# u of batches 2 to 7 as seven half-size products; one buffer for w_out and the weight sums, refilled from a DRAM copy; x's sums in the gates' place

## The chip, the core and the metric

The kernel runs on one core of a Trainium2 chip. The metric is the device time of one execution in microseconds (us), taken as the median of several runs. Five engines work side by side: PE (matrix products, with its weight loads shown as PEld), DVE (VectorE), ACT (ScalarE), POOL (GpSimd) and SP (SyncE, which here only issues transfers). Each runs its own instructions in a fixed order and waits on semaphores for the others.

## What is computed

Attention without a softmax, then a gated feed-forward block, all in float32:

```python
kv = einsum('bhsd,bhse->bhde', k, v)          # 8 batches, 8 heads, 576 x 64
out = einsum('bhsd,bhde->bhse', q, kv)
x = out / sqrt(mean(out**2, -1) + 1e-6) * g_norm   # then laid out as [8, 576, 512]
h = maximum(x @ w_in, 0)                      # w_in 512 x 1024
u, v = h[..., :512], h[..., 512:]
v_n = (v - mean(v)) / sqrt(var(v) + 1e-6)
v_s = einsum('ts,bsd->btd', w_spatial, v_n) + b_spatial[None, :, None]
result = (u * v_s) @ w_out                    # w_out 512 x 512
```

## The kernel before

**Precision by splitting.** For batches 1 to 7 every large matrix is held as a high part and a low part in a reduced format (names end in H and L: `XH`, `XL`, `WIH`, `WIL`, `VH`, `VL`, `GH`, `GL`, `WOH`, `WOL`). A product is then three PE products, high times high, high times low, low times high (`hl`, L286). A split is two instructions (`split`, L319): ACT copies the value to the high part, DVE subtracts that from the value and writes the low part. Batch 0 is computed in plain float32 by lines of its own while the weights arrive.

**Stages of a batch.** 576 tokens are four tiles of 128 and a tail of 64, the tail being treated together with that of the neighbouring batch. `hv` (L307) makes v for one tile, 12 products of 512 columns; `hv_end` (L325) applies the relu on ACT, the layer norm (statistics and scaling on DVE) and the split, and `sums` (L338) forms sums of V's quarters on DVE. `u_unit` (L408) makes a 128 x 288 block of u: for each of the four 128-row pieces of the contraction three products of 288 columns, 12 in all, in one PSUM bank, from which ACT writes the relu into `U`. There are 8 such units in a batch, 96 products. `sp_steps` (L453) is the spatial product, already in the seven-product (Strassen-Winograd) form, 14 steps over two halves `q`, with `tail_product` for the tail; `gate` (L434) multiplies with `U` on DVE and splits the result into `GH` and `GL`. `out_unit` (L511) multiplies with w_out, and ACT and SP carry the result out.

**Attention between.** `first` (L762: hv and u), `second` (L782: spatial) and `last` (L788: out) call `step` (L706) between their units; each `step` runs one piece of the attention of the next batches (`att_k`, `att_qa`, `att_t`). `att_qa` squares on ACT and sums per head on DVE (`norm_a`, L181: one 512-wide square, then a `TENSOR_REDUCE`); batch 0's first units use the other form in it, eight 64-wide squares on ACT that also accumulate, and no reduction.

**Order and buffers.** A scheduler places the instructions of each engine from the program order and the dependencies. PSUM banks for `hv`, `u`, spatial and out come from one pool of four (`ps_mm`), the attention's from another of three. `WIH`/`WIL` hold w_in for the whole run, `WOH`/`WOL` w_out, `GH`/`GL` the gates. All transfers are issued by SP.

## Time and profile before

| | |
|---|---|
| median of 3 runs | 517.86 us (517.69 to 518.56) |
| the profiled execution's own time | 517.55 us |
| its span, first to last instruction | 515.8 us |
| granted PE clock, mean over the span | 0.999 |
| PE busy | 505.7 us, 98% of the span |
| DVE busy | 359.9 us, 70% |
| ACT busy | 236.4 us, 46% |
| POOL busy | 8.5 us |

The span is covered by PE nearly without a gap from 86 us on. The first 86 us are batch 0 and the decoding of the weights, the stretch from 86 to 164 us is batch 1, and from there each batch takes 54 to 64 us according to how much attention lies in it. "Busy" of DVE and ACT counts time in which at least one instruction is in flight; the instructions of one engine overlap a little, so that a sum of single durations is larger than the busy time.

### The profile page before, as it was taken

How to read it: one execution, taken by the hardware profiler on the slowest of the kernel's cores; microseconds unless marked ns; L12 is line 12 of the kernel's file. 1: busy time of each engine (PE TensorE's matmuls, PEld its weight loads, DVE VectorE, ACT ScalarE, POOL GpSimd, SP SyncE). 2: the span in 40 equal slices, each digit the busy share in tenths (PEclk: the TensorE clock that was granted, in tenths of full speed). 3: DMA queues.
4: the chain of work that ended last, by engine and by line, in shares of the span. 5: the costliest groups of instructions: out<-in, count | busy, mean ns of one | idle time of the engine just before them, and what ended most of it. 6: DMA issues, size and time to landing. Idle time of an engine off the chain costs nothing.

```text
span 515.8 us, 9316 instructions
## 1 busy us (share of the span) xinstructions
PE 505.7 (98%) x3508; PEld 447.5 (87%) x3508; DVE 359.9 (70%) x1076; ACT 236.4 (46%) x572; POOL 8.5 (2%) x23
## 2 busy tenths in 40 slices
PE   7999999999999999999999999999999999999996
PEld 6648777898988899889998899989998899988995
DVE  3898599798952889556692698818694488938470
ACT  2555455865533465335443366325442356434321
POOL 5000000000000000000000000000000000000000
PEclk9999999999999999999999999999999999999999
DMA  8995300423253002112416301220223201020003
GB/s 258 328 323 186 104 24 1 154 67 114 103 191 116 1 1 65 68 39 93 144 35 199 110 22 56 83 104 21 80 80 138 69 0 43 2 81 1 1 0 102
DMA packets 22303, 46.48 MB, mean 90 GB/s; under 512 B 2866, under 2 KB 7474, under 8 KB 22260
## 3 DMA queue, kind: packets, MB, share of 16 engines
q1 hardware_dynamic: 22260, 45.91, 27.5%
q8 instruction: 27, 0.44, 0.4%
q14 instruction: 16, 0.13, 0.1%
HBM read 36.46 MB, written 9.44 MB: 89 GB/s over the span
## 4 chain that ended last, share of the span: by engine, by line
PE 91%; DMA 3%; ACT 3%; DVE 2%; issue 1%; SPq 0%; ACTq 0%
PE pso L284 19%; PE psu L284 16%; PE psh L317 14%; PE psb L423 6%; PE pso L204 5%; PE psc L423 4%; PE psa L423 4%; PE pskv L129 4%; PE psu L391 3%; PE pstr L232 2%; PE psa L400 2%; DMA stage<-w_in 2%; PE psh L367 2%; PE psh L284 2%; PE pst L157 1%; DMA KV<-kvm 1%
## 5 line engine op out<-in xcount | busy, mean ns | idle before, releaser
L284 PE MATMUL psu<-XH,WIH 128*128 128x288 f32 x224 | 66.6, 297 | 0.4 <-ACT U L414 0.4
L284 PE MATMUL psu<-XL,WIH 128*128 128x288 f32 x224 | 66.1, 295 | 0.0
L284 PE MATMUL psu<-XH,WIL 128*128 128x288 f32 x224 | 66.0, 295 | 0.0
L284 PE MATMUL pso<-WOH,GH 128*128 128x512 f32 x144 | 57.0, 398 | 0.0
L284 PE MATMUL pso<-WOL,GH 128*128 128x512 f32 x144 | 56.6, 393 | 0.0
L284 PE MATMUL pso<-WOH,GL 128*128 128x512 f32 x144 | 53.8, 396 | 0.0
L450 ACT CAST GH<-g 128x288 fp32r<-128x288 f32 (+2 forms) x84 | 26.6, 350 | 45.7 <-DVE g L442 45.3
L296 DVE BATCH_NORM_STATS2 s<-v 128x6 f32<-128x512 f32 x32 | 22.0, 692 | 35.8 <-ACT v L290 35.7
L317 PE MATMUL psh<-WIL,XH 128*128 128x512 f32 x112 | 43.7, 391 | 0.0
L317 PE MATMUL psh<-WIH,XH 128*128 128x512 f32 x112 | 43.7, 395 | 0.0
L317 PE MATMUL psh<-WIH,XL 128*128 128x512 f32 x112 | 43.3, 391 | 0.0
L284 PEld LDWEIGHTS psu<-XH,WIH 128*128 128x128 f32 x224 | 42.0, 188 | 1.0 <-ACT U L414 0.6
L284 PEld LDWEIGHTS psu<-XL,WIH 128*128 128x128 f32 x224 | 42.1, 188 | 0.3
L284 PEld LDWEIGHTS psu<-XH,WIL 128*128 128x128 f32 x224 | 42.0, 188 | 0.0
L191 DVE TENSOR_REDUCE ss<-x 128x8 f32<-128x512 f32 x38 | 25.9, 683 | 18.4 <-ACT x L190 18.2
L321 DVE TENSOR_TENSOR VL<-v,VH 128x512 fp32r<-128x512 f32 (+1 forms) x56 | 33.9, 620 | 5.1 <-ACT VH L320 4.6
L414 ACT ACTIVATE U<-psu 128x288 f32<-128x288 f32 x56 | 22.8, 412 | 29.1 <-PE psu L284 28.1
L320 ACT CAST VH<-v 128x512 fp32r<-128x512 f32 (+1 forms) x56 | 30.5, 564 | 11.5 <-DVE v L343 5.8
L524 ACT COPY o<-pso 128x512 f32<-128x512 f32 x35 | 19.7, 589 | 35.1 <-PE pso L284 27.8
L284 PEld LDWEIGHTS pso<-WOH,GL 128*128 128x128 f32 x144 | 27.0, 188 | 5.7
L284 PEld LDWEIGHTS pso<-WOL,GH 128*128 128x128 f32 x144 | 27.1, 188 | 5.0
L284 PEld LDWEIGHTS pso<-WOH,GH 128*128 128x128 f32 x144 | 27.0, 188 | 4.7
(188 smaller groups left out, 1204.1 us busy)
## 6 DMA issues: line engine op xcount, KB each, us to landing
KV<-kvm SPq DMA_DIRECT2D x31, 512.0 KB, 4.9
out<-o SPq DMA_DIRECT2D x32, 256.0 KB, 2.2
qt<-qT SPq DMA_DIRECT2D x16, 288.0 KB, 2.9
stage<-w_in SPq DMA_DIRECT2D x8, 512.0 KB, 6.3
qt<-qT SPq DMA_DIRECT2D x16, 256.0 KB, 2.7
KT<-kvt SPq DMA_DIRECT2D x32, 64.0 KB, 4.7
stage<-w_out SPq DMA_DIRECT2D x4, 512.0 KB, 5.7
stage<-wsT SPq DMA_DIRECT2D x4, 288.0 KB, 4.4
```

Of the source, the lines that this page charges most:

```text
L129: return nc.tensor.matmul(ps[h:h + D, at:at + D], of[:, 0, h:h + D], of[:, 1, h:h + D], start=c == 0, stop=c == NC)
L191: nc.vector.tensor_reduce(ss, heads(x), axis=AX.X, op=ALU.add)
L204: nc.tensor.matmul(ps[:, c * P:(c + 1) * P], qt[:, c * P:(c + 1) * P], st[p], start=True, stop=True)
L284: nc.tensor.matmul(ps, lt, rh, start=i == 0, stop=i == n - 1)
L296: nc.vector.bn_stats(s6, v)
L317: nc.tensor.matmul(ps, lt, rh, start=k == 0 and i == 0, stop=k == NP - 1 and i == 2)
L320: nc.scalar.copy(hi, x)
L321: nc.vector.tensor_tensor(lo, x, f32(hi), op=ALU.subtract)
L414: nc.scalar.activation(U[:, d, cols], ps[:, 0:HS], AF.Relu)
L423: nc.tensor.matmul(ps, lt, rh, start=start and i == 0, stop=stop and i == len(pairs) - 1, skip_group_check=True)
L450: nc.scalar.copy(GH[:, d, dst], g[:, src])
L524: nc.scalar.copy(o, ps)
```

## The change

u of batches 2 to 7 is made by the seven-product scheme that the spatial product has: x (as two by two blocks, halves of the contraction by halves of the tokens) times w_in's u half (as two by two blocks). A step takes 6 products of 288 columns (two 128-row pieces by three), and 14 steps make a batch: 84 products where there were 96.

- Weights. `WIH`/`WIL` are divided into `WVH`/`WVL` (v half) and `WUH`/`WUL` (u half, four blocks). `w_sums` forms the four weight sums once, in batch 1 (two calls): on DVE from high and low part, split again; one sum takes the place of a block no longer needed, three go to DRAM (`spare_u`, 1.57 MB) by SP.
- One buffer `WO` for two uses. w_out's parts are also written to DRAM (`spare_o`, 2.10 MB). In each batch from 2 on, `to_u` takes the buffer under the name `UX` and loads `spare_u` as two transfers of 0.79 MB; `to_out` takes it back and loads `spare_o` as two transfers of 1.05 MB. These four transfers a batch are issued by POOL.
- x's sums. `x_sums` forms per batch, on DVE, 8 additions of high and low part and 8 additions or subtractions, and splits four sums of two pieces each (8 ACT copies, 8 DVE subtractions). They lie in `T`, which has the place of the gates' buffer `G`, and in the rest of `UX`. `T` may be written when the last `out_unit` of the batch before has read `G`, and `G` again when u has read `T`. The tails of the gates move to a small buffer `GT`.
- u's steps. Per batch 4 ACT copies (two of `p1`, two of a finished block) and 10 DVE sums out of PSUM take the place of 8 relus on ACT. A bank is used by up to three steps: its next products wait until the DVE sum that reads the last ones is done. The relu is done in `gate`: `max(U, 0) * v_s` in one instruction.
- Moved from DVE to ACT: the scaling of the layer norm in `hv_end` (with one small DVE product more), the tails' `TB` copies, and for batches 2 to 7 the sums of squares in `att_qa`, now the accumulating form, eight squares and no reduction.

```diff
 def att_q(b, p, st):
-        att_qa(b, p, st)
+        att_qa(b, p, st, b > 1 and True)
...
-        layer_norm(ps, v, nc.vector)
+        layer_norm(ps, v, nc.scalar)
...
+    def x_sums_():
+        for k in range(2):
+            q = []
+            for of, j, name in ((0, 0, "p1"), (2, 1, "u2"), (0, 1, "u3"), (2, 0, "g")):
+                q.append(work.tile([P, HS], F32, name=name, tag=name))
+                x = [f32(x[:, of + k, j * HS:(j + 1) * HS]) for x in (XH, XL)]
+                nc.vector.tensor_tensor(q[-1], *x, op=ALU.add)
+            q11, q22, q12, q21 = q
+            nc.vector.tensor_tensor(q11, q12, q11, op=ALU.subtract)
+            nc.vector.tensor_tensor(q12, q22, q12, op=ALU.subtract)
+            nc.vector.tensor_tensor(q22, q22, q11, op=ALU.subtract)
+            nc.vector.tensor_tensor(q21, q21, q22, op=ALU.subtract)
+            for n, x in (1, q22), (0, q11), (2, q12), (3, q21):
+                split(TH[n][:, k], TL[:, n, k], x)
...
+        def p1(q):
+            ps = bank(q, "a")
+            u_product(ps, q, 0, 0)
+            nc.scalar.copy(temp(q, "p1"), ps)
+        def p2(q):
+            ps = st.pop((q, "a"))
+            u_product(ps, q, 1, 1, False)
+            nc.scalar.copy(own(q, 0, 0), ps)
+        def p6(q):
+            ps = bank(q, "b")
+            u_product(ps, q, 3, 4)
+            nc.vector.tensor_tensor(temp(q, "u2"), ps, st[q, "p1"], op=ALU.add)
+        def p5(q):
+            ps = bank(q, "c")
+            u_product(ps, q, 6, 3)
+        def p7(q):
+            ps = st[q, "b"]
+            u_product(ps, q, 4, 5, False)
+            nc.vector.tensor_tensor(temp(q, "u3"), ps, st[q, "p1"], op=ALU.add)
+            nc.vector.tensor_tensor(own(q, 1, 1), st[q, "c"], st.pop((q, "u3")), op=ALU.add)
+        def p4(q):
+            ps = st.pop((q, "b"))
+            u_product(ps, q, 2, 6, False)
+            nc.vector.tensor_tensor(own(q, 1, 0), ps, st.pop((q, "p1")), op=ALU.add)
+        def p3(q):
+            ps = st.pop((q, "c"))
+            u_product(ps, q, 5, 2, False)
+            nc.vector.tensor_tensor(own(q, 0, 1), ps, st.pop((q, "u2")), op=ALU.add)
...
-        nc.vector.tensor_tensor(g, ps, U[:, d, cols], op=ALU.mult)
+        nc.vector.scalar_tensor_tensor(g, U[:, d, cols], 0.0, ps, op0=ALU.max, op1=ALU.mult)
...
+    def to_u():
+        t = pool_g.tile([P, 7, 2, HS], F32R, name="T", tag="G")
+        x = pool_o.tile([P, 12 * HF + S], F32R, name="UX", tag="WO")
...
+        for i in range(2):
+            nc.gpsimd.dma_start(UX[:, i], spare_u[:, i])
+    def to_out():
+        main_g()
+        main_o()
+        for i in range(2):
+            nc.gpsimd.dma_start(WO[:, i], spare_o[:, i])
...
     def first(b):
+        if b > 1:
+            to_u()
+            x_sums()
         for c in (0, 2, 1, 3):
             hv(b, c)
             step()
...
+        for n, f in enumerate(u_steps()):
...
+        to_out()
```

**How the instructions stand.** On PE, where u of batch 6 ends and the spatial product begins, before:

```order
L284 MATMUL psu<-XH,WIH 128x288
L284 MATMUL psu<-XL,WIH 128x288
L284 MATMUL psu<-XH,WIL 128x288
L423 MATMUL psa<-WSH,VH 128x288
L423 MATMUL psa<-WSL,VH 128x288
```

and on PE in the second half of u of batch 6, with the change (`psua`, `psub`, `psuc` are the banks of the three step families):

```order
L544 MATMUL psua<-XH,WUL 128x288
L544 MATMUL psub<-T,WUL 128x288
L544 MATMUL psuc<-T,UX 128x288 x6
L544 MATMUL psub<-T,WUH 128x288 x2
L544 MATMUL psub<-T,WUL 128x288
L544 MATMUL psub<-T,WUH 128x288 x2
L544 MATMUL psub<-T,WUL 128x288
L544 MATMUL psub<-T,UX 128x288 x6
L544 MATMUL psuc<-T,UX 128x288 x6
L544 MATMUL psub<-T,UX 128x288 x6
L544 MATMUL psub<-UX,WUH 128x288
```

Three products a piece in an unbroken row of 96 have become steps of six on banks that several steps share, and these banks now pass through DVE and ACT between two steps.

On ACT, in u of batch 6, before (from the relu of v's last tiles on; `psu` is u's bank):

```order
L290 ACTIVATE v<-psh 128x512
L166 ACTIVATE sv<-mv,epsc 128x1
L290 ACTIVATE v<-psh 128x512
L414 ACTIVATE U<-psu 128x288
L166 ACTIVATE sv<-mv,epsc 128x1
L320 CAST VH<-v 128x512
L414 ACTIVATE U<-psu 128x288 x2
L362 CAST TA_90<-v 64x512
L362 CAST TA_91<-v 64x512
```

and with the change (`psua` is the bank of the first step families, `x,ss<-pso` one accumulating square):

```order
L499 COPY p_5365<-psua 128x288
L295 ACTIVATE v<-psh 128x512
L504 COPY U<-psua 128x288
L192 ACTIVATE x,ss<-pso 128x64 x6
L171 ACTIVATE sv<-mv,epsc 128x1
L192 ACTIVATE x,ss<-pso 128x64
L171 ACTIVATE sv<-mv,epsc 128x1
L192 ACTIVATE x,ss<-pso 128x64 x8
L171 ACTIVATE sh<-ss,epsc 128x8
L504 COPY U<-psua 128x288
```

Between the two copies out of `psua` now stand fifteen squares of two attention units and three square roots.

On DVE, where the gates of batch 6 end and the layer norm of batch 7 begins, before:

```order
L451 TENSOR_TENSOR GL<-g,GH 128x64
L196 TENSOR_TENSOR x<-pso,rh 128x512
L440 TENSOR_TENSOR g<-psc,u_5200 128x288
L451 TENSOR_TENSOR GL<-g,GH 128x288
L442 TENSOR_TENSOR g<-g,U 128x288
L451 TENSOR_TENSOR GL<-g,GH 128x224
L451 TENSOR_TENSOR GL<-g,GH 128x64
L226 SCALAR_TENSOR_TENSOR XL<-pstr,gcol,XH 128x512
L296 BN_STATS s_5381<-v 128x6
L297 BN_AGGR mv<-s_5381 128x2
```

and with the change (`p`, `u` and `g` without `psc` are x's sums):

```order
L438 TENSOR_TENSOR u_5855<-XH,XL 128x288
L441 TENSOR_TENSOR u_5837<-u_5835,u_5837 128x288
L441 TENSOR_TENSOR u_5857<-u_5855,u_5857 128x288
L326 TENSOR_TENSOR G<-g,G 128x224
L326 TENSOR_TENSOR GT<-g,GT 128x64
L442 TENSOR_TENSOR u_5835<-u_5835,p_5833 128x288
L442 TENSOR_TENSOR u_5855<-u_5855,p_5853 128x288
L438 TENSOR_TENSOR g<-XH,XL 128x288
L443 TENSOR_TENSOR g<-g,u_5835 128x288
L443 TENSOR_TENSOR g<-g,u_5855 128x288
L301 BN_STATS s_5888<-v 128x6
L302 BN_AGGR mv<-s_5888 128x2
```

x's additions have come in between the last gates and the first statistics; the eight subtractions that write `T` stand some 20 rows further down, behind the statistics of v's second tile. On POOL the two transfers into `UX`, the copy of x's tail that was there before (in even batches) and the two into `WO` follow each other.

## Rows read from the trace of the kernel before

**Rows 1.** The page, busy time of each engine (share of the span) and instructions.

```profile
PE 505.7 (98%) x3508; PEld 447.5 (87%) x3508; DVE 359.9 (70%) x1076; ACT 236.4 (46%) x572; POOL 8.5 (2%) x23
```

**Rows 2.** Waits of PE over the whole span: us in total, times, longest.

```profile
PE pskv L129 <- DMA KV<-kvm: 2.1, 2, 1.8
...
PE psu L284 <- ACT U L414: 0.4, 1, 0.4
```

**Rows 3.** Busy us (and instructions) in the stretches of batches 4 to 7.

```profile
283.40:342.64 59.24, 59.24 (x408) 54.47 (x407) 43.61 (x136) 27.86 (x65) 0.40 (x1) 1.00 0.24 78
342.64:404.28 61.64, 61.64 (x484) 56.44 (x483) 39.51 (x121) 25.40 (x61) 0.00 (x0) 1.00 0.25 78
404.28:461.21 56.93, 56.93 (x361) 52.37 (x361) 43.74 (x135) 27.75 (x64) 0.40 (x1) 1.00 0.09 29
461.21:515.80 54.59, 50.64 (x305) 45.92 (x303) 27.72 (x79) 18.29 (x44) 0.00 (x0) 0.99 0.10 34
```

**Rows 4.** The same by stage: out of batch 6, then hv, u, spatial of batch 7.

```profile
449.80:461.20 11.40, 11.40 (x58) 9.61 (x57) 5.58 (x19) 3.83 (x9) 0.00 (x0) 1.00 0.13 47
...
461.21:472.11 10.90, 10.90 (x51) 9.02 (x50) 6.68 (x24) 4.18 (x9) 0.00 (x0) 1.00 0.13 48
472.11:484.82 12.71, 12.71 (x98) 12.71 (x98) 9.43 (x25) 6.54 (x15) 0.00 (x0) 1.00 0.00 0
484.82:500.39 15.57, 15.57 (x112) 15.15 (x111) 9.74 (x26) 4.52 (x13) 0.00 (x0) 1.00 0.00 1
```

**Rows 5.** Pieces of the chain that ended last: start us, us, what.

```profile
439.12 0.89 PE pso L204 x8
...
461.21 10.89 PE psh L317 x48
472.11 12.72 PE psu L284 x96
```

**Rows 6.** Groups by form: count, busy us, mean ns, idle before and its end.

```profile
L191 DVE TENSOR_REDUCE ss<-x 128x8 f32<-128x512 f32 x38 | 25.9, 683 | 18.4 <-ACT x L190 18.2
...
L414 ACT ACTIVATE U<-psu 128x288 f32<-128x288 f32 x56 | 22.8, 412 | 29.1 <-PE psu L284 28.1
...
L442 DVE TENSOR_TENSOR g<-g,U 128x288 f32<-128x288 f32 x42 | 19.0, 453 | 0.5
...
L190 ACT ACTIVATE x<-pso 128x512 f32<-128x512 f32 x31 | 18.4, 599 | 12.1 <-PE pso L204 10.8 <-PE pstr L232 1.1
...
L300 DVE TENSOR_SCALAR v<-v,mv,rv 128x512 f32<-128x512 f32 x32 | 17.3, 543 | 0.7
```

**Rows 7.** DVE in order of time, a stretch without idle time: start, us.

```profile
444.34 0.45 DVE L476 TENSOR_TENSOR u<-psb,p 128x288 f32<-128x288 f32 x1
444.71 0.45 DVE L442 TENSOR_TENSOR g<-g,U 128x288 f32<-128x288 f32 x1
...
446.18 0.68 DVE L196 TENSOR_TENSOR x<-pso,rh 128x512 f32<-128x512 f32 x1
446.78 0.68 DVE L191 TENSOR_REDUCE ss<-x 128x8 f32<-128x512 f32 x1
447.37 0.45 DVE L442 TENSOR_TENSOR g<-psa,U 128x288 f32<-128x288 f32 x1
```

**Rows 8.** ACT in order of time: eight accumulating squares, first and next instruction after them.

```profile
19.32 0.22 ACT L187 ACTIVATE x<-pso 128x64 f32<-128x64 f32 x1 [0.60 <-PE pso L204]
19.44 0.19 ACT L187 ACTIVATION_READ_ACCUMULATOR x<-pso 128x1 f32 x1
...
21.09 0.30 ACT L166 ACTIVATE sh<-ss,epsc 128x8 f32<-128x8 f32 x1
```

**Rows 9.** Transfers of the whole run: queue and bytes, then two kinds with landing times.

```profile
q1 hardware_dynamic: 22260, 45.91, 27.5%
...
KV<-kvm SPq DMA_DIRECT2D x31, 512.0 KB, 4.9
...
qs<-qT SPq DMA_DIRECT2D x16, 64.0 KB, 2.0
```

More of the change, by code (lines that the diff above doesn't have):

```diff
@@ L338, in sums, with add_up @@
     def sums(k, first, second):
+        add_up(first, second)
+        for x, n in (first, 3), (second, 5):
+            split(VH[:, k, n:n + 2], VL[:, k, n:n + 2], x.rearrange("p (h f) -> p h f", f=HF))
+    def add_up(first, second):
         a11, a21, a12, a22 = first[:, 0:HF], first[:, HF:FH], second[:, 0:HF], second[:, HF:FH]
@@ L344, in sums @@
         nc.vector.tensor_tensor(a12, a12, a11, op=ALU.subtract)
-        for x, n in (first, 3), (second, 5):
-            split(VH[:, k, n:n + 2], VL[:, k, n:n + 2], x.rearrange("p (h f) -> p h f", f=HF))
     def hv_tail():
@@ new lines, in w_sums @@
+    def w_sums(kk):
+        first, second = (work.tile([P, FH], F32, name="v", tag="v", bufs=3) for _ in range(2))
+        for x, n, step in (first, 0, 3), (second, 1, 1):
+            of = [w[:, kk, n:n + step + 1:step] for w in (WUH, WUL)]
+            nc.vector.tensor_tensor(x.rearrange("p (h f) -> p h f", f=HF), f32(of[0]), f32(of[1]),
+                                    op=ALU.add)
+        add_up(first, second)
+        split(WUH[:, kk, 3], WUL[:, kk, 3], first[:, 0:HF])
+        for x, n in (first[:, HF:FH], slice(0, 1)), (second, slice(1, 3)):
+            parts = [work.tile([P, DM], F32R, name="w", tag="stg", bufs=2) for _ in range(2)]
+            parts = [w.rearrange("p (n f) -> p n f", f=HF)[:, 0:n.stop - n.start] for w in parts]
+            split(*parts, x.rearrange("p (n f) -> p n f", f=HF))
+            for i, w in enumerate(parts):
+                nc.sync.dma_start(spare_u[:, i, kk, n], f32(w))
@@ new lines, in u_product @@
+    def u_product(ps, q, n, of, start=True, stop=True):
+        cols = slice(q * P, (q + 1) * P)
+        raw = {0: (0, 0), 1: (2, 0), 2: (2, 1)}
+        pairs = []
+        for k in range(2):
+            if n < 4:
+                w = [x[:, k, n, cols] for x in (WUH, WUL)]
+            else:
+                w = [UX[:, i, k, n - 4, cols] for i in range(2)]
+            if of in raw:
+                at, j = raw[of]
+                x = [x[:, at + k, j * HS:(j + 1) * HS] for x in (XH, XL)]
+            else:
+                x = [TH[of - 3][:, k], TL[:, of - 3, k]]
+            pairs += hl(*w, *x)
+        multiply(ps, pairs, start, stop)
@@ L416, in product, with multiply @@
     def product(ps, q, n, of, start=True, stop=True):
         cols = slice(q * P, (q + 1) * P)
-        pairs = [m for k in range(2) for m in hl(VH[:, k, n, cols], VL[:, k, n, cols],
-                                                 WSH[:, k, of], WSL[:, k, of])]
+        multiply(ps, [m for k in range(2) for m in hl(VH[:, k, n, cols], VL[:, k, n, cols],
+                                                      WSH[:, k, of], WSL[:, k, of])], start, stop)
+    def multiply(ps, pairs, start, stop):
@@ L441, in gate @@
             ps = g
-        nc.vector.tensor_tensor(g, ps, U[:, d, cols], op=ALU.mult)
+        nc.vector.scalar_tensor_tensor(g, U[:, d, cols], 0.0, ps, op0=ALU.max, op1=ALU.mult)
         if j == 0:
-            parts = [(slice(0, HS), cols)]
-        else:
-            n = NT - HS
-            parts = [(slice(0, n), slice(HS, NT)),
-                     (slice(n, HS), slice(TAILC[i], TAILC[i] + TAIL))]
-        for src, dst in parts:
-            nc.scalar.copy(GH[:, d, dst], g[:, src])
-            nc.vector.tensor_tensor(GL[:, d, dst], g[:, src], f32(GH[:, d, dst]), op=ALU.subtract)
+            split(GH[:, d, cols], GL[:, d, cols], g)
+            last_gate[0] = next(i for i in reversed(nc.cur_bb.bb.instructions) if i.engine == mybir.EngineType.DVE)
+        else:
+            n, own = NT - HS, slice(i * TAIL, (i + 1) * TAIL)
+            split(GH[:, d, HS:NT], GL[:, d, HS:NT], g[:, 0:n])
+            split(GT[:, 0, d, own], GT[:, 1, d, own], g[:, n:HS])
     def sp_steps(b):
@@ L791, in last @@
             step()
+            if b == 1 and c == 1:
+                w_sums(1)
     first(1)
```

113 lines of the change are left out of this document (83 added, 30 removed).

## The prediction

> **What bounds the kernel now.** I read the page's busy times first: PE is busy 98% of the span, DVE 70%, ACT 46% [rows 1]. Then PE's waits: the longest kind is 2.1 us, for the first key transfers, and u waits 0.4 us in all for ACT's relu [rows 2]. Then the batches one by one: in batches 4 to 6 PE is busy for the whole of each stretch, to the hundredth [rows 3]. So in the steady part the time is the number of PE products times their spacing, and everything else hides under it. The spacing is read from the chain of waits: 96 products of 288 columns in 12.72 us are 132.5 ns each, 48 of 512 columns in 10.89 us are 227 ns, an attention unit of four float32 products is 0.89 us [rows 5]. The granted clock is 1.00 in these stretches [rows 3], its upper level, and PE never pauses there, so it has no part in what follows.
>
> How much room the other engines have is read from the same table. In the fullest stretch, batch 6, DVE is busy 43.7 of 56.9 us and ACT 27.8 [rows 3]. Inside batch 7, DVE has 5.6 of 11.4 us in the out stage before it, 6.7 of 10.9 in hv, 9.4 of 12.7 in u and 9.7 of 15.6 in the spatial stage [rows 4].
>
> **What the change takes from PE.** Each batch from 2 to 7 has 84 products of 288 columns for u in place of 96. No other product is added or removed. The operands have the same shapes (128 x 128 weights, 288 moving columns), so 6 x 12 = 72 products leave at 132.5 ns: 9.54 us, 1.59 us a batch. This lies on the path in full.
>
> **What it adds to DVE.** Durations overlap on one engine, so I take distances from start to start: a 288-wide instruction of 0.45 us is followed after 0.37, a 512-wide one after 0.60 [rows 7]. Per batch come 16 additions for x's sums, 8 subtractions for their low parts and 10 sums out of PSUM, 34 of 288 columns: 34 x 0.37 = 12.6 us. Four products of one column for the scaling on ACT lie between nothing and the 0.37 of a 288-wide one; I take 0.2 each, 0.8 us. Four scalings leave (0.54 less the overlap of 0.08: 4 x 0.46 = 1.8 us) and four reductions (0.68, start to start 0.60: 2.4 us) [rows 6, 7]. The tails' copies leave too and are not counted. The relu in the gate replaces a product of the same size; I cost it at nothing, between 0.37 and 0.45 either way. Net 12.6 + 0.8 - 1.8 - 2.4 = 9.2 us more a batch. Batch 6 comes to 52.9 of 55.3 us, batch 4 to 52.8 of 57.6, batch 5 to 48.7 of 60.0. On average it fits. Locally it is nearly full: in the out stage of batch 6 the 16 additions for batch 7 bring 5.9 us to the 5.6 there, 11.5 of 11.4; hv and u of batch 7 together go from 16.1 to 16.1 + 18 x 0.37 + 0.8 - 1.8 = 21.8 of 22.0 us. The spatial stage after it keeps nearly 6 us of room.
>
> **What it adds to ACT.** Eight accumulating squares take from 19.32 to 21.09, 1.77 us [rows 8], in place of one square of about 0.5: 4 x 1.27 = 5.1 us. Four scalings of 0.5, eight high parts of 0.3 and four copies for eight relus of 0.3 (all durations of rows 6 less 0.1 of overlap) give 2.0 + 2.4 - 1.2. Net 8.3 us, 36 of 55 in batch 6. ACT has room; what counts is the queue. In u of batch 6 fifteen squares and three square roots stand before the copy that frees the bank for the second p5. From the end of the first attention unit on, ACT needs 15 x 0.22 + 3 x 0.30 + 0.4 = 4.6 us [rows 6, 8]; PE has one more unit and 30 products before p5, 0.89 + 3.98 = 4.9 us. It fits by 0.3 us; were it late by as much, the three even batches would lose 0.9 us together, and if the scaling and the roots wait for DVE in between, 1 us each.
>
> **What waits for DVE.** Six links a batch now go PE to DVE to PE: u2, u3 and one finished block for each q must be read before the bank's next step. Behind a waiting DVE instruction stand V's splits, the attention's norms and the gates, in one queue. Two sums show the room. In batch 6, from the end of the first p6 to the first spatial product that needs V's last low part, PE has 16.2 us of work (counted from the order with the spacings above) and DVE 30 wide and 14 one- to eight-column instructions (these at 0.1 to 0.2 each), 14.9 to 16.3 us. In batch 5 the same stretch has 16.7 us on PE and 13.9 to 15.3 on DVE, but there DVE also stands waiting at six sums for a product to end, some 2 us by laying the rows side by side, so that the last low part comes about 0.5 us late. Bounds: 0 a batch (every place fits), 1.6 a batch (the whole gain). I take 0.5 us a batch, 3.0 in all, since two of three places looked at fit and one misses by that.
>
> **Transfers.** They must land between the last reading of the place and the first use. From the order this room on PE is, for `UX`, 9.4 us in batch 7 (24 products of 512, 30 of 288) and 15 to 20 in the others; for `WO`, 11.0 in batch 7 (83 products), 12.1 in batches 3 and 5, 13.7 to 15 else. The trace has no transfer issued by POOL; all 45.9 MB go through SP's queue [rows 9]. The nearest rows are 512 KB in 4.9 us and 64 KB in 2.0 [rows 9]. At 512 KB in 4.9 with the two halves moving side by side, as the keys' pairs do, `UX` takes 7.3 us and `WO` 9.8: both fit, with 2.1 and 1.2 us to spare in batch 7. One half after the other they take 14.7 and 19.6: then `UX` is 5.3 late in batch 7, and `WO` 4.6 to 8.6 in every batch, 39 in all. I take the first, to which the pairs are nearer, and cost the transfers at nothing; 44 us is the far end.
>
> By the Trainium skill (page "DMA: Bandwidth & Descriptors", section on the anatomy of a GpSimd transfer) such a transfer takes about 2.0 us and its bytes at 436 GB/s. An estimate from that page would be 5.6 us for `UX` and 6.8 for `WO`, and the sum would stay as it is; no run here shows it yet.
>
> **The rest.** The weight sums and the copies to DRAM come once, beside batch 1: two calls of some nine wide DVE instructions, at most 2 x 9 x 0.60 = 11 us in a stretch where PE does not wait for them, and 16 more transfers on SP, past which the next keys and queries are queued. I take 0.3 us, bounds 0 and 1.5.
>
> **Sum.** The profiled execution took 517.55 us: 1.75 outside its span and 0.31 under the median of the runs. 517.55 - 9.54 + 3.0 + 0.3 = 511.3; on the scale of the median 511.6 us.
>
> **Rivals.** First, everything hides: 517.86 - 9.54 = 508.3. For it speaks that PE shows no gap with DVE at 77% in batch 6; against it that DVE comes to 96%.
>
> Second, DVE's links bind. Each sum out of PSUM stands in a queue with 512-wide pieces of 0.60; if three of the six links a batch come late by one such piece, a batch loses 1.8 us, six lose 10.8, and the time is 517.86 - 9.54 + 10.8 + 0.3 = 519.4, slower than before. It decides from 1.6 us a batch. For it: the fill computed above. Against: the rows on PE between a sum and its reader are another step of 0.8 us at each place.
>
> Third, the transfers are late, by descriptors, by the DVE, or one behind the other. Landing half way between the two bounds (`UX` 11, `WO` 14.7) would cost 1.6 in batch 7 for `UX`, and for `WO` 2.6 twice, 1.0 and 3.7, together 11.5: 517.86 - 9.54 + 11.5 + 3.3 = 523.1. PE would stand before the first out product.
>
> The Trainium skill has a rule that speaks for this third case (page "SBUF — State Buffer", sections on the two separate sides and on who interferes): descriptors of a GpSimd transfer are written by GpSimd through a port pair that DVE locks while it runs a copy or scalar operation in its two-port mode; it advises the other queues. The scaling, such an operation, leaves DVE with this change for v's four tiles, and subtractions of two tensors are not among those the page names for writing. By that rule the third case stays the unlikely one; no run here shows it yet.
>
> **Chances.** Forecast (509.5 to 514): 0.50. Everything hides (under 509.5): 0.14. The links cost 1 to 1.5 us a batch (514 to 516.8): 0.10. The links bind (516.8 to 520): 0.15, of which 0.08 within 0.2% of before and 0.07 above. Late transfers: 0.11. A difference of 0.2%, 1.0 us, is about what a measurement of this kernel tells from none. Faster by more 0.74, within it 0.08, slower 0.18. The range 508.0 to 518.5 leaves out late transfers and the upper part of the binding links, some 0.17.
>
> **What would show it.** PE with 72 products fewer at the same 132 ns; DVE busy near 52 us in batch 6's stretch and about 415 in all; waits of PE on DVE or ACT, none before, of some 3 us in all at `psub`, `psuc` and the first spatial steps; no wait on a transfer at the first use of `UX` and `WO`. Wrong would be: a wait of whole microseconds at the out stage's first product (transfers), waits at each `psub` step (links), or another spacing of u's products.

## The result and the profile after

The changed kernel takes 512.93 us (median of 6 runs, 511.76 to 514.52), the kernel before 518.44 beside it; the ratio is 0.9900, with an interval of 0.9881 to 0.9919. (Ratios are of the means of the fast executions; one execution of the kernel before took 1019.29 us and is left out of them.) The prediction was 511.6, in a range of 508.0 to 518.5. The profiled execution of the changed kernel took 512.66 us, with a span of 510.9; that of before 517.55. So 4.9 us are gained where the sum said 6.2.

First the page, the line that answers to [rows 1]: busy us, share of the span and instructions of each engine.

```profile
PE 498.2 (98%) x3436; PEld 437.9 (86%) x3436; DVE 412.3 (81%) x1266; ACT 291.0 (57%) x1006; POOL 21.5 (4%) x47
```

3436 products for 3508: 72 have gone. DVE comes to 412.3 us, forecast at about 415 (more on that below). PE's busy time falls by 7.5 us and not by 9.54, and its waits behind 86 us, below (us in total, times, longest), come to only 1.2 us, where before had one of 0.4 [rows 2]. Something is missing in both views.

```profile
PE pstt L247 <- DVE x L201: 0.6, 1, 0.6
PE pstr L237 <- DVE qh L173: 0.4, 1, 0.4
PE psu L289 <- ACT U L425: 0.2, 1, 0.2
```

It hides between products. Here are PE's rows in batch 4's spatial stage (start, us busy):

```profile
322.07 0.29 PE L544 MATMUL psb<-WSL,VH 128*128 128x288 f32 x1
322.20 0.30 PE L544 MATMUL psb<-WSH,VL 128*128 128x288 f32 x1
322.56 0.40 PE L544 MATMUL psb<-WSH,VH 128*128 128x288 f32 x1
```

The third starts 0.36 us after the second and not 0.13. The second counts as busy for 0.30 of it, so that the table of waits says nothing and the busy time swallows it. What shows such losses is the distance from start to start. So I took, for each kernel, the start of every product less the sum of the distances that the products ahead of it should have (0.2277 us for 512 columns, 0.1325 for 288, 0.112 for 128, 0.0367 for 64, 0.2425 for those of 65 rows): the time that PE has lost until then. What this loss grew by, stretch by stretch (the stretches fit the changed kernel's stages and are cut at the same times, in us from the span's start, in every line; the last column is the sum):

```
              to 80  80-160 160-190 190-210 210-310 310-340 340-430 430-460 460-end    sum
before        32.40    3.17   -0.01    0.02    0.37    0.18    0.21    0.08    0.23  36.65
after         32.73    5.11    0.06    1.12    0.36    0.73    0.19    0.65    0.30  41.25
before_84     32.73    3.26   -0.01    0.02    0.28    0.15    0.15    0.20    0.47  37.25
cut_w         32.70    4.25    0.04    0.91    0.33    0.76    0.17    0.66    0.28  40.10
cut_x         32.08    4.99    0.04    0.88    0.33    0.74    0.14    0.67    0.25  40.12
cut_sq        32.86    4.37    0.04    1.38    0.34    0.54    0.19    0.46    0.29  40.47
cut_links     32.07    5.55    0.06    0.35    0.33    0.48    0.16    0.38    0.29  39.67
cut_all       32.34    3.46    0.01    0.35    0.29    0.47    0.11    0.40    0.23  37.66
```

The first two lines are the result (the others belong to the experiments). 80 to 160 us is batch 1 with its neighbours, 190 to 210, 310 to 340 and 430 to 460 are the spatial stages of batches 2, 4 and 6. Against before, the changed kernel loses 0.33 us more in the prologue, 1.94 in batch 1, 0.07 up to the end of batch 2's u (160-190), nothing in u of the others or in the odd batches, and in the three even spatial stages 1.10 + 0.55 + 0.57 = 2.22. With the other stretches 4.60 in all. -9.54 + 4.60 = -4.94, and 517.55 - 4.94 is 512.61, where 512.66 was measured. A later start shifts work over the border at 80 us: counted from the same product on (the first of batch 1's hv), the prologue has 0.45 and batch 1 1.79.

The other engines, between the first products of u of batch 4, 5, 6 and 7 (start and end; us; PE, PEld, DVE, ACT, POOL busy; granted clock, DMA share, GB/s), first before, then after:

```profile
294.70:353.41 58.71, 58.71 (x403) 53.94 (x402) 43.12 (x130) 27.46 (x64) 0.40 (x1) 1.00 0.18 58
353.41:415.95 62.54, 62.54 (x491) 57.28 (x490) 41.21 (x130) 26.57 (x64) 0.00 (x0) 1.00 0.25 80
415.95:471.94 55.99, 55.99 (x353) 51.53 (x352) 42.04 (x129) 26.57 (x61) 0.40 (x1) 1.00 0.09 29
```

```profile
295.43:354.20 58.77, 58.71 (x401) 53.60 (x400) 49.70 (x166) 38.67 (x168) 2.51 (x5) 1.00 0.39 131
354.20:413.61 59.41, 59.41 (x465) 54.11 (x464) 48.48 (x149) 31.53 (x99) 2.12 (x4) 1.00 0.41 136
413.61:468.57 54.96, 54.91 (x342) 49.98 (x340) 47.68 (x151) 34.63 (x132) 2.52 (x5) 1.00 0.25 84
```

DVE has 6.6, 7.3 and 5.6 us more, ACT 11.2, 5.0 and 8.1. DVE is not full over a batch (47.7 of 55.0 in batch 6, forecast 52.9 of 55.3), but nearly so in the spatial stages. The same view there, batches 1, 2, 3, 4, 6 and 7:

```profile
131.68:147.74 16.06, 15.33 (x144) 14.34 (x142) 15.99 (x44) 8.51 (x20) 0.00 (x0) 1.00 0.38 132
194.43:210.68 16.25, 15.78 (x149) 14.96 (x147) 16.02 (x47) 9.15 (x42) 1.68 (x3) 1.00 0.50 180
254.45:266.81 12.36, 12.36 (x126) 12.12 (x124) 11.77 (x37) 4.79 (x14) 1.06 (x2) 1.00 0.53 185
313.19:328.86 15.67, 15.61 (x149) 14.98 (x147) 15.15 (x46) 8.19 (x34) 1.46 (x3) 1.00 0.47 166
...
431.37:445.51 14.14, 14.09 (x108) 13.70 (x107) 13.63 (x41) 7.40 (x32) 1.46 (x3) 1.00 0.41 149
480.89:491.91 11.02, 11.02 (x85) 11.02 (x84) 8.54 (x22) 3.22 (x9) 1.06 (x2) 1.00 0.53 190
```

In batches 1, 2, 4 and 6 DVE is busy for 96 to 100% of the stage, and PE loses time there; in batch 3 for 95%, and PE loses nothing. Shares so close to each other don't show a cause by themselves.

Last the transfers, as in [rows 9] (queue and bytes; then KB each and median us from issue to landing), and below them the second halves of batch 7's two reloads alone:

```profile
q0 software_dynamic: 3456, 22.02, 12.5%
...
WO<-spare_o POOLq DMA_DIRECT2D x12, 1024.0 KB, 6.3
UX<-spare_u POOLq DMA_DIRECT2D x12, 768.0 KB, 6.0
```

```profile
UX<-spare_u POOLq DMA_DIRECT2D x1, 768.0 KB, 6.8
...
WO<-spare_o POOLq DMA_DIRECT2D x1, 1024.0 KB, 7.3
```

The two halves of a reload are issued 0.52 us apart (once 0.66) and move side by side, and the second one lands last: the medians over both halves say too little. A pair is there 7.0 to 7.6 us (`UX`) and 7.7 to 9.2 us (`WO`) after the first issue, in batch 7 after 7.34 and 7.79. There, in the tightest batch, 8.84 us pass from the first issue to the first product that reads `UX`, and 10.45 for `WO`. PE waits for neither anywhere.

### The profile page after: what moved, and what is told of

Read it like the earlier page. It is cut to its first block, busy times and chain, and to the rows that moved or that the text cites. A ratio compares the mean times of both kernels' runs of the same rounds, so it can differ in the third digit from the quotient of the medians.

```text
span 510.9 us, 9902 instructions
## 1 busy us (share of the span) xinstructions
PE 498.2 (98%) x3436; PEld 437.9 (86%) x3436; DVE 412.3 (81%) x1266; ACT 291.0 (57%) x1006; POOL 21.5 (4%) x47
## 4 chain that ended last, share of the span: by engine, by line
PE 72%; DVE 11%; ACT 7%; DMA 7%; SPq 1%; issue 1%; ACTq 0%; DVEq 0%
PE pso L289 18%; PE psh L322 12%; PE psb L544 4%; PE psub L544 4%; PE psc L544 4%; PE pskv L134 4%; PE psua L544 3%; DMA KV<-kvm 3%; PE psu L400 3%; PE pso L209 3%; PE psa L409 2%; PE psa L544 2%; PE psuc L544 2%; PE pstr L237 2%; PE psu L289 2%; DMA qt<-qT 2%
## 5 line engine op out<-in xcount | busy, mean ns | idle before, releaser
L289 PE MATMUL pso<-WO,G 128*128 128x512 f32 x384 | 97.2, 396 | 0.0
L289 PEld LDWEIGHTS pso<-WO,G 128*128 128x128 f32 x384 | 70.3, 188 | 14.1
L192 ACT ACTIVATE x<-pso 128x64 f32<-128x64 f32 x200 | 42.8, 254 | 5.6 <-PE pso L209 5.5
L322 PE MATMUL psh<-WVL,XH 128*128 128x512 f32 x112 | 43.7, 390 | 0.0
L322 PE MATMUL psh<-WVH,XH 128*128 128x512 f32 x112 | 43.5, 393 | 0.0
L322 PE MATMUL psh<-WVH,XL 128*128 128x512 f32 x112 | 43.4, 392 | 0.0
L192 ACT ACTIVATION_READ_ACCUMULATOR x<-pso 128x1 f32 x200 | 42.0, 239 | 0.0
L544 PE MATMUL psb<-WSH,VH 128*128 128x288 f32 x84 | 25.4, 304 | 0.3
L309 ACT ACTIVATE v<-v,mv,rv 128x512 f32<-128x512 f32 x28 | 23.3, 837 | 3.1 <-DVE mv L308 3.1
L544 PE MATMUL psb<-WSL,VH 128*128 128x288 f32 x84 | 24.6, 295 | 0.0
```

What stands on the lines that cost most here:

```text
L192: nc.scalar.activation(x[:, cols], ps[0:rows, cols], AF.Square, accum_out=ss[:, h:h + 1])
L289: nc.tensor.matmul(ps, lt, rh, start=i == 0, stop=i == n - 1)
L309: nc.scalar.activation(v, v, AF.Identity, bias=m, scale=r)
L322: nc.tensor.matmul(ps, lt, rh, start=k == 0 and i == 0, stop=k == NP - 1 and i == 2)
L544: nc.tensor.matmul(ps, lt, rh, start=start and i == 0, stop=stop and i == len(pairs) - 1, skip_group_check=True)
```

## What could have cost the 4.6 us, and how it was tried

My theory after the comparison: the added work stands in DVE's and ACT's queues ahead of what PE waits for, the weight sums in batch 1, and in the even batches x's sums, the squares on ACT or the readers of u's banks. The rival: PE's new row of products, which the planner laid anew over the whole program, waits by its own order (the planner is the scheduler that places each engine's instructions). First I left parts out in the source, which lets the planner set the order anew. Then, when that turned out to change more than the part, I left the order alone and cut the finished program.

**The products alone.** The kernel before with 12 products fewer a batch:

```diff
-        three(ps[:, 0:HS], [m for k in range(NP) for m in
+        few = NP - (b > 1 and j)
+        three(ps[:, 0:HS], [m for k in range(few) for m in
```

> The kernel before, with 12 of the 96 products for u left out in each of batches 2 to 7 (the last of four k in the four second halves), so that u lacks a part of its sum, and nothing else changed. It measures what 72 products fewer are worth without any of the additions. Theory (product bound, 132.5 ns each): 9.54 us under the kernel before, ratio 0.9816. Rival (other engines or transfers come due when PE is faster): less than 9.0 us, with new waits of PE behind 160 us.

508.93 us, ratio 0.9829 (0.9814 to 0.9845). That is 8.9 us with an interval of 8.0 to 9.6. In its line of the table above PE loses 0.60 more than before, 0.33 of it in the prologue, which this edit doesn't touch. The 8.9 lies just under the 9.0 that was to part theory and rival, and the interval holds both; what decides is the trace. Behind 160 us no new wait of weight appears, so the rival falls, and the price of 132.5 ns a product holds, with the spread of the prologue on top.

**The weight sums moved, and the weight sums left out.** Two kernels, from the source:

```diff
-            if b == 1 and n == 13:
-                w_sums(0)
...
-            if b == 1 and c == 1:
-                w_sums(1)
+            if b == 1 and c < 2:
+                with tc.issue_after(end_gate[0]):
+                    w_sums(c)
```

> The changed kernel, with the weight sums of both halves moved behind the last gate of batch 1, into its out stage, where they share the vector engine with x's sums for batch 2. Theory (the weight sums stand in DVE's queue among the gates of batch 1's spatial stage, and PE waits for the gates): the 1.3 us that PE loses between 143 and 146 us goes, PE shows no wait at `pstt` there, and the median falls from 512.9 to about 511.5 us. Rival (the loss in that stage comes from the gate itself, which now holds the relu, or from the order of the attention's steps): 512.9 us, and the waits stay where they are. A third way out: batch 1's out stage is too full then, the first hv products of batch 2 or its p6 wait, and the time stays near 512.9 with the wait in another place.

```diff
     def w_sums(kk):
 
+        for i, w in enumerate((WUH, WUL)):
+            nc.sync.dma_start(spare_u[:, i, kk], f32(w[:, kk, 0:3]))
+        return
```

> The changed kernel without the arithmetic of the weight sums: raw blocks of the weights are copied to DRAM in their place (four transfers for eight), so that u is multiplied with other weights. Left out: the sums of w_in's blocks and their splits, about 20 wide instructions on DVE and 6 on ACT. Theory (the weight sums cost the 1.7 us that PE loses between 130 and 160 us): 511.2 us, and what PE has lost by 160 us is within 0.7 us of the kernel before. Rival (the links and gates cost it): 512.9 us.

The first took 526.52 us, ratio 1.0170 (1.0153 to 1.0187), slower than the kernel before. The second 513.46, ratio 0.9916 (0.9902 to 0.9930): no gain, though the arithmetic was gone. The largest part of what the first lost shows in its longest wait of PE and in ACT in order of time:

```profile
PE psh L322 <- ACT o L648: 5.4, 1, 5.4
```

```profile
171.87 0.58 ACT L648 COPY o<-pso 128x512 f32<-128x512 f32 x1 [1.07 <-DVE v L355]
...
177.91 0.58 ACT L648 COPY o<-pso 128x512 f32<-128x512 f32 x1 [2.09 <-DMA spare_u<-w]
```

The parts of the weight sums and the output tiles share one ring of two buffers (the tag `stg`). In the out stage the output copies stand between the weight sums: the trace puts the first down to a weight sum on DVE (line 355), the second to a weight part on its way to DRAM. Until the first has run the PSUM banks stay full, and PE stands for 5.4 us before batch 2's hv; behind it 1.8 us more go by the lower clock (last section). The rest of the 13.5 us that the profiled run is longer than the changed kernel is spread over smaller waits of the new order, for copies on ACT (3.1) and for keys (1.6) among others. In the changed kernel the weight parts are copied on ACT at 138.65 and 141.27, between output copies at 135.13 and 156.07, and no output waits for them. The other run, without the arithmetic, lost its time in a new place. ACT, and PE:

```profile
134.68 0.48 ACT L595 COPY p<-psa 128x288 f32<-128x288 f32 x1
```

```profile
135.21 0.41 PE L547 MATMUL psa<-WSH,VH 128*128 128x288 f32 x1 [0.95 <-ACT p L595]
```

In the changed kernel the same copy stands so:

```profile
133.48 0.48 ACT L592 COPY p<-psa 128x288 f32<-128x288 f32 x1
```

It comes 1.2 us later without the sums, behind much the same instructions, and PE's new row no longer has the four transposes (`pstr`) that stand ahead of this step in the changed kernel: PE is there as early and waits 0.95 us. A run with another order says nothing about the cost of what was left out. So the theory was neither confirmed nor refuted by these two.

**x's sums left out in the source.**

```diff
-            x_sums()
...
-            if of in raw:
+            if True:
-                at, j = raw[of]
+                at, j = raw[of % 3]
```

> The changed kernel without x's sums: the products for u take raw blocks of x in their place, so that nothing writes the sums' buffer. Left out: 16 additions, 8 subtractions (DVE) and 8 casts (ACT) a batch, about 8.9 us of DVE. All products, links and reloads stay. Theory (in batches 2, 4 and 6 DVE is full in the spatial stage and PE waits there, 1.1 + 0.5 + 0.5 us; x's sums push the work of the out and hv stages into it): these waits fall to under 0.5 us in all, 511.0 us. Rival (the waits are of that stage's own order, with what stands there in DVE's queue, and x's sums are long done by then): 512.9 us, same waits. In batch 1 nothing changes in either case but the end of its out stage.

518.52 us, ratio 1.0011 (0.9999 to 1.0022): 48 us of DVE fewer in all (364.1 for 412.3), and the whole gain lost. Again by the order: a wait of 1.9 us in the u stage of batch 2, for the relu of hv on ACT that empties a bank, and several shorter ones. What that wait did to the clock is told further down.

**The finished program cut.** From here on the planner's result stands as it is, every instruction in its row with its waits. After planning, chosen instructions are replaced by themselves on fewer columns (the squares of a unit by one instruction, those behind it dropped where nobody counts on them):

```diff
+def less(ap, few=8):
...
+    return copy.replace(ap, ap=p[:-1] + [[p[-1][0], few]])
...
+        if i.name in CUT:
+            by[i.name] = copy.replace(i, outs=tuple(less(x) for x in i.outs),
+                                      ins=tuple(less(x) if is_ap(x) else x for x in i.ins))
...
-            x_sums()
+            with marked(nc):
+                x_sums()
```

> The changed kernel's finished program, with every instruction in its place and with its waits; only the weight sums' instructions on DVE and ACT work on 8 columns of each block in place of 256, and the transfers to DRAM carry raw blocks of the weights. Left out: nearly all of the weight sums, some 10 us of DVE beside batch 1. Theory (the gates of batch 1's spatial stage stand behind them in DVE's queue): the 1.3 us that PE loses between 143 and 146 us go, what PE has lost by 160 us falls from 37.8 to about 36.4, and the median is about 511.5. Rival (that loss is of the stage's own order, or of ACT's squares): 512.9 us, with the wait at `pstt` where it was.

> The same finished program, order and waits; only x's sums and their splits work on 8 columns in place of 288 (32 instructions on DVE and 8 on ACT in each batch from 2), and the products that read the sums read a part of the spatial weights, so that u is another. Left out: some 8 us of DVE in each batch. Theory A (in batches 2, 4 and 6 DVE is behind from the out and hv stages on, and so late in the spatial stage): PE's loss there, 1.1 + 0.5 + 0.5 us, falls under 0.5 in all, the median to about 511. Theory B (the loss is made inside the spatial stage, where a split of x waits on DVE for its high part, which stands on ACT behind eight squares): 512.9 us and the same losses.

> The same finished program, order and waits; of the eight squares on ACT of each attention unit from batch 2 on, the first is one square of eight columns into the eight sums' places, and those behind it are left out, or are of one column where another engine counts on them, so that the normalization is another. Left out: about 1.4 us of ACT a unit, 5.6 a batch. Theory B (the split of x waits for its high part behind the squares): PE's loss in the spatial stages of batches 2, 4 and 6 falls from 2.1 us to under 0.7, the median to about 511.5; in batch 1 the loss shrinks as well if ACT has a part in it. Theory A (DVE's load): the losses stay, 512.9.

> The same finished program, order and waits; only the instructions that read u's banks (ten sums on DVE and four copies on ACT in each batch from 2) work on 8 columns in place of 288, so that u keeps stale values. Left out: 10 x 0.33 us of DVE and 4 x 0.25 of ACT a batch. The forecast's term (0.5 us a batch for the links): PE would gain up to 3.0 us, the median 510. What the trace of the changed kernel says (PE loses next to nothing inside u, another step stands in between): a gain under 0.7 us, 512.2 to 512.9, and what there is of it in the spatial stages behind u.

The medians and ratios: `cut_w` 511.67, 0.9887 (0.9871 to 0.9903); `cut_x` 512.90, 0.9911 (0.9894 to 0.9927); `cut_sq` 511.18, 0.9885 (0.9856 to 0.9914); `cut_links` 511.31, 0.9879 (0.9864 to 0.9894). The intervals overlap with that of the changed kernel, so the verdicts rest on the table of PE's losses above. How far that can be trusted shows in what must be equal: up to 80 us the six programs that run the same row lost between 32.07 and 32.86, a scatter of 0.8 us (the first transfers decide there: PE waited 3.5 us for keys in the changed kernel's run and 2.2 in `cut_x`'s); in the three even stages together `cut_w`, which changes nothing there, lost 2.33 where the changed kernel lost 2.50. Firmer than these sums is one place at a time: the same product in the row, in all the runs, with its distance and the one behind it, which a pause makes longer too.

- In the even stages x's sums cost nothing: 2.29 without them. Theory A falls.
- The squares cost nothing that can be told: 2.38. Batches 4 and 6 gain 0.2 each by their absence, and batch 2 loses 0.3. Theory B falls too, for these stages.
- The readers of u's banks cost 1.29: 1.21 are left of 2.50, so the forecast's 3.0 was too much and the "under 0.7" of the trace too little. They are cut inside u, and the gain comes behind it: the places at `pstr` in batch 2 (0.64) and at V's last low part in batches 4 and 6 (0.15 and 0.16) go to nothing, and in none of the three other cuts do they. PE's waits of that run behind 86 us no longer have the one at `pstr`:

```profile
PE pstt L307 <- DVE x L261: 0.6, 1, 0.6
PE psu L349 <- ACT U L485: 0.2, 1, 0.2
PE pstr L297 <- DVE x L261: 0.2, 1, 0.2
```

DVE in order of time in the changed kernel shows the queue that ends in it. PE waits until 197.88 for `qh`:

```profile
195.87 0.44 DVE L529 TENSOR_TENSOR U<-psuc,u 128x288 f32<-128x288 f32 x1
196.23 0.41 DVE L352 TENSOR_TENSOR v<-v 128x256 f32<-128x256 f32 x1
...
197.05 0.68 DVE L201 TENSOR_TENSOR x<-pso,rh 128x512 f32<-128x512 f32 x1
197.65 0.19 DVE L173 RECIPROCAL qh<-ah 128x8 f32<-128x8 f32 x1
```

The last sum of u, some of V's block sums and an attention unit's normalization come one after the other, and PE is already in the spatial stage.

- In batch 1, `cut_w` loses 0.86 less and `cut_sq` 0.74 less than the changed kernel. But `cut_x` and `cut_links`, which run the same there until x's sums for batch 2, lie 0.56 apart (4.99 and 5.55), so neither sum settles it. Three places do. The products that wait for `psb` at 143.96 and at `pstt` at 145.87 lose 0.35 to 0.41 and 0.77 in the changed kernel and in all single cuts but `cut_w`; there, and with all four cut, they lose 0.00 and 0.26. So the weight sums cost 0.9 at these two. The u product that waits for a relu on ACT at 107.57 loses 0.45 to 0.47, and nothing in the two runs without the squares. The kernel before lost 0.63 at the same product, though; with two further waits for ACT the changed one loses 1.05 in this u stage, so that 0.4 is new there. The rows of the changed kernel, DVE, and PE behind it:

```profile
142.25 0.68 DVE L452 TENSOR_TENSOR v<-WUH,WUL 128x512 f32<-128x512 f32 x1
142.85 0.68 DVE L326 TENSOR_TENSOR w<-v,w 128x512 fp32r<-128x512 f32 x1
143.46 0.45 DVE L613 TENSOR_TENSOR u<-psb,p 128x288 f32<-128x288 f32 x1
...
144.71 0.42 DVE L352 TENSOR_TENSOR v<-v 128x256 f32<-128x256 f32 x1
145.04 0.68 DVE L201 TENSOR_TENSOR x<-pst,rh 128x512 f32<-128x512 f32 x1
```

```profile
144.98 0.29 PE L552 MATMUL psb<-WTL,TB 128*128 128x288 f32 x1
145.87 0.63 PE L247 MATMUL pstt<-ident,x 128*128 128x128 f32 x4 [0.59 <-DVE x L201]
```

Two wide pieces of the weight sums stand ahead of the sum that frees `psb`, and another ahead of the `x` for which PE waits 0.59 us. With the weight sums cut, DVE is there first and waits for PE:

```profile
142.75 0.46 DVE L676 TENSOR_TENSOR u<-psb,p 128x288 f32<-128x288 f32 x1 [1.13 <-PE psb L607]
```

**All four cuts at once.**

> The changed kernel's finished program, order and waits once more, with all four cuts at once: weight sums, x's sums, the squares of the attention units and the readers of u's banks, each left out as where it was cut alone, so that nearly all that the change adds on DVE and ACT is gone, and more. Theory (the 4.6 us that PE lost beyond the kernel before are the added work in DVE's and ACT's queues, at the end of u and in the spatial stages of batches 1, 2, 4 and 6): what PE loses from 80 us on falls from 8.5 us to within 0.6 of the kernel before's 4.25 us, and the median is 508.5 to 509.3 us. Rival (a good part of the loss is the new row of the products itself, which stands in another order and waits by it whatever the others do): PE still loses over 1.5 us more than the kernel before from 80 us on, and the median stays above 510.

509.28 us, ratio 0.9829 (0.9813 to 0.9845), the same ratio as the products alone. Its page has DVE below the kernel before:

```profile
PE 497.2 (98%) x3436; PEld 438.0 (86%) x3436; DVE 351.7 (69%) x1266; ACT 242.3 (48%) x696; POOL 21.3 (4%) x47
```

From 80 us on PE loses 5.32 us, where the changed kernel loses 8.52 and before 4.25. So 3.20 of the 4.27 us are the added work, batch 1 in nearly all of its share (3.46 against 3.17 in before). 1.07 stay, which is more than the 0.6 that I allowed and less than the rival's 1.5. They lie in the even spatial stages, 0.94 (1.22 for before's 0.28, the same as with the readers of u's banks alone cut), and in batch 1, 0.29; the other stretches lose a little less than before. Most of the 0.94 is one place in each of the three stages, with 0.29, 0.27 and 0.27: the first product of a `psb` step that waits for the sum on DVE that reads the bank. In batch 4, on ACT, DVE and PE:

```profile
317.36 0.69 ACT L296 ACTIVATE XH<-pstr,gcol 128x512 fp32r<-128x512 f32 x1 [1.60 <-PE pstr L303]
```

```profile
318.08 0.75 DVE L297 SCALAR_TENSOR_TENSOR XL<-pstr,gcol,XH 128x512 fp32r<-128x512 f32 x1 [0.42 <-ACT XH L296]
...
318.82 0.45 DVE L684 TENSOR_TENSOR u<-psb,p 128x288 f32<-128x288 f32 x1
```

```profile
319.33 0.40 PE L615 MATMUL psb<-WSH,VH 128*128 128x288 f32 x1
```

ACT and DVE both stood idle before; what they do here the kernel before does too, and none of it was moved or added. The scaling and the tails' copies don't stand in this chain. But between `p7`, the step whose bank is read, and `p4`, which needs it next, PE now has only the other half's `p7`, 0.8 us, where the kernel before had 3 us of other products in this stage. So here the rival is right: the new row of the products costs some 0.8 us. That is read from the rows; no run tried the old row at this place.

**Sums on GpSimd.** If DVE's queue is the trouble, some of it can go to an engine that is idle:

```diff
-        add_up(first, second)
+        add_up(first, second, nc.gpsimd)
...
-    def add_up(first, second):
+    def add_up(first, second, eng):
...
-        nc.vector.tensor_tensor(a22, a21, a22, op=ALU.add)
+        eng.tensor_tensor(a22, a21, a22, op=ALU.add)
```

> The changed kernel with the eight 256-wide sums of V's blocks of each batch on GpSimd in place of DVE; the planner sets the order anew. DVE has 8 x 0.33 = 2.6 us less a batch, just ahead of the spatial stage, where PE loses 1.1 + 0.7 + 0.5 us in batches 2, 4 and 6 (a copy of 256 columns on GpSimd took 0.40 us in the trace of the changed kernel). Theory (DVE's queue at the end of u and in the spatial stage is what PE waits for; with the link sums cut that loss had halved): 511.0 to 511.9 us. Rival (the sums take over 0.6 us each on GpSimd, or stand there behind the reload that waits for PE, and V's last low parts come later): 513.5 us or more, with waits at the first spatial products that read them.

> The changed kernel with all sums of the weights (twelve of 256 and 512 columns) on GpSimd; their splits stay on ACT and DVE, and the planner sets the order anew. Theory (the weight sums' share of the loss in batch 1, 0.9 us where they were cut to 8 columns): 511.9 to 512.3 us, if the new order has no other wait. Rival (the weights reach DRAM later, the first reload waits for them): a wait of PE at batch 2's first products with `UX`, 514 us or more.

> Both together: V's sums and the weights' sums on GpSimd. If the gains add up: 510.3 to 511.3 us, better than the changed kernel by 0.3 to 0.5%. Rival as for each alone: 513 us or more.

527.58 us, ratio 1.0181 (1.0155 to 1.0207); 513.85, 0.9912 (0.9897 to 0.9926); 525.06, 1.0134 (1.0117 to 1.0151). V's sums are far slower there. The groups on GpSimd (count, busy us, mean ns), and the longest wait of PE behind the prologue:

```profile
L355 POOL TENSOR_TENSOR v<-v 128x256 f32<-128x256 f32 x14 | 11.4, 811 | 1.1
```

```profile
PE psb L544 <- ACT VH L325: 1.5, 1, 1.5
```

0.77 to 0.81 us each in a chain of four is 3.1 us, where DVE takes one every 0.33, 1.3 in all; V's last splits come later, and PE waits for them, as the rival said; but that is 2.1 of some 9 us of waits, and the others lie at a dozen other places, so this order too is another program, and no clean price of the engine. The weights' sums alone gave nothing either: the new order has the same wait of 0.95 us for the copy `p` in batch 1 as the run without them. Both together (525.06) are slow like the first. None of the kernels that compute the whole of it beats the changed one.

## Why the prediction was right, step by step

- **The products**: 72 x 132.5 ns. Right: u's 504 products in batches 2 to 7 stand 131 to 133 ns apart (medians by bank), and the products alone gave 8.9 us with 9.54 inside the interval.
- **DVE's load**: 9.2 us more a batch forecast, 6.5 measured on average of three, 7.7 over all six (from the first hv product of batch 2 on 281.3 us, before 235.3), so 1.5 to 3 us too high. That the total of 412.3 lies near the forecast 415 is luck: the 415 had left out the weight sums, and batch 1 has 6.2 us more. Over the batch it fits, as said; "nearly full locally" was right for the wrong stage: from the first out product of batch 6 to the last (445.51 to 463.12) DVE has 15.0 of 17.6 us, the spatial stage of batch 6 13.63 of 14.14. "Nearly 6 us of room" there was read from batch 7 [rows 4], which has less attention beside it; in the even batches the kernel before had 1.3 to 3.0.
- **ACT's load**: 8.3 us forecast, 8.1 measured on average.
- **The links**: 3.0 us in all forecast, at `psub`, `psuc` and the first spatial steps. The 2.2 that the even stages lost lie near it by luck: the readers of u's banks make 1.29 of them, and most of the others is PE's new row, which the sum didn't have. Inside u PE loses nothing, since another step of 0.8 us stands in each place. The loss comes behind u, where the last readers delay what follows them in DVE's queue. And I had it in the wrong batches. In batch 6 the count itself was right: 30 wide and 14 small instructions take 16.13 us until V's last low part is there, and PE loses 0.16 at it; but another 0.31 is lost at the `psb` step, behind what I had counted. In batch 5 that low part is there at 373.98, and PE reads it at 374.50, 0.5 us early where 0.5 late was forecast.
- **The even batches' ACT queue**, said to fit by 0.3 us: it fits. PE has no wait at the second p5.
- **The transfers**, costed at nothing: right. Of `UX`'s room in batch 7 (9.4 us forecast, 8.84 there) 1.5 are left, of `WO`'s (11.0 and 10.45) 2.7. The halves move side by side, as I took it; 7.3 us from the keys' rate was right for `UX` (7.0 to 7.6), 9.8 too long for `WO` (7.7 to 9.2). The estimate from the Trainium skill (page "DMA: Bandwidth & Descriptors", section on the anatomy of a GpSimd transfer) was 5.6 and 6.8, and the trace doesn't agree: it has 1.4 to 2.0 us more for the first and 0.9 to 2.3 more for the second. The page gives its sum for one transfer, and here two follow each other. The rule of its page "SBUF — State Buffer" (section "Who interferes with whom"), by which DVE could hold up the descriptors, shows in no wait of PE: each half of `UX` landed within 4.9 to 6.9 us, in all 12 cases, before its first use. Whether it has a part in these times no run here shows.
- **The rest**, the term that failed: 0.3 us with an upper bound of 1.5, measured 0.33 in the prologue and 1.94 in batch 1. The prologue's part is within its scatter of 0.8. For batch 1 I had written that the weight sums stand "in a stretch where PE does not wait for them". They stand in the spatial stage of batch 1, in which DVE is busy 15.99 of 16.06 us, and cost 0.9 us of waits there; and the squares of the attention units for batches 2 and 3, which I had counted for the later batches only, stand in ACT's queue in batch 1's u. With both cut (and the rest of the four) that stretch loses 0.29 more than before.

The rivals: everything hides (508.3) is what `cut_all` comes near to (509.28), not the kernel. Links that bind at every step were refuted by the u stages, late transfers by the landings. The sum came out 1.3 us low on the profiled execution (511.3 and 512.66), which is the missing 1.6 of batch 1, less the 0.8 too much for the links, and the prologue. That it came so near owes something to luck: of 3.3 us of losses in the sum, 1.29 came by the way that I had given.

## What to carry over

A wait shorter than the busy time of the instruction ahead of it is in no table of waits: compare distances from start to start. Where a planner sets the order, leaving a part out in the source measures another program; cut the finished one, and compare it product by product, since sums over a stretch scatter by some tenths. And work that "comes once" is not cheap by that: look at which stage it lands in, and whether the engine is full just there, in each batch and not in one.

## What the runs showed of the hardware

TensorE's clock, after a wait. In the run without x's sums PE waited 1.9 us and went on at 185.56:

```profile
185.56 0.40 PE L544 MATMUL psub<-XH,WUH 128*128 128x288 f32 x1 [1.90 <-ACT v L295]
```

The stretches before the wait, then soon after it and behind that, read in the same columns as above:

```profile
178.00:183.60 5.60, 5.60 (x38) 5.09 (x36) 4.53 (x20) 2.98 (x7) 0.00 (x0) 1.00 0.01 1
...
186.30:189.70 3.40, 3.40 (x16) 3.40 (x15) 3.06 (x19) 3.40 (x33) 0.00 (x0) 0.50 0.00 0
189.70:193.00 3.30, 3.30 (x26) 3.30 (x26) 2.99 (x11) 3.29 (x13) 0.00 (x0) 1.00 0.00 0
```

For 3.4 us the granted clock is 0.50, the lower level, and the products of 288 columns start every 0.24 us and not every 0.1325: 14 of them start in it, 0.11 us each, 1.5 us more, so that the wait cost nearly twice its length. After the wait of 5.4 us in the run with the moved weight sums the products of 512 columns ran at 0.43 us apart, at the same level:

```profile
172.50:176.20 3.70, 3.69 (x9) 2.92 (x10) 2.28 (x7) 1.37 (x4) 0.00 (x0) 0.50 0.37 130
```

After the wait of 0.95 us in the run without weight sums the clock stayed at 1.00.

DVE and GpSimd hold each other up. In the run with V's sums on GpSimd a split on DVE that takes 0.42 us took 0.91 beside such a sum; in 4 of the 14 splits of that form it was 0.54 to 0.91. DVE and then GpSimd:

```profile
116.35 0.91 DVE L326 TENSOR_TENSOR VL<-v,VH 128x256 fp32r<-128x256 f32 x1
```

```profile
116.24 0.74 POOL L352 TENSOR_TENSOR v<-v 128x256 f32<-128x256 f32 x1 [107.80 <-DVE VL L326]
```

The split ends at 117.26, 0.28 after the sum's end at 116.98; in the three other slow cases it is 0.27 to 0.28 as well, and each time the sum had started first. In the three cases in which the split started first it took its 0.42, and the sum 0.77 to 0.99 where 0.73 is usual. The Trainium skill (page "SBUF — State Buffer", section "Who interferes with whom") says that a DVE instruction with two inputs in SBUF contends with a GpSimd instruction that reads SBUF; the trace agrees.
